# Linear attention and a two-layer MLP on one core: q of batch 2, its four tiles and block 0's outputs placed anew

## The chip, the cores and the metric

The kernel runs on one core of one Trainium2 chip, in one launch. The metric is the device time of one execution in microseconds, as the median of several. A core has TensorE (PE in the profile; its weight loads are PEld), VectorE (DVE), ScalarE (ACT), GpSimd (POOL) and SyncE (SP), each with its own in-order queue of instructions, and 16 DMA engines, which the queues of SyncE, ScalarE and GpSimd feed.

## The reference

Per batch and head, `kv = k^T v` and `out = q kv`, normalised by its root mean square over the head and scaled by `g_norm`. The heads side by side give `x` with 512 columns; after a layer norm it goes through two matrices with a ReLU between, and `x` is added. There are 8 batches, 8 heads, 576 rows, head size 64 and 2048 hidden columns.

```
kv  = einsum('bhsd,bhse->bhde', k, v)
o   = einsum('bhsd,bhde->bhse', q, kv)
x   = o / sqrt(mean(o*o, -1) + 1e-6) * g_norm       # then heads side by side
xn  = (x - mean(x)) / sqrt(var(x) + 1e-6) * g_ln
out = x + relu(xn @ w_ch1) @ w_ch2
```

## The kernel before

Each batch gives a block of 512 rows, in four tiles of 128; the last 64 rows of all batches make a ninth block, "rem". Tile (b, j) below is the j-th tile of batch b.

**A block's matrices.** `mm1` (L680) multiplies the block's turned x, `xT_blk`, by w1 and ScalarE stores the ReLU as `m1` (L693). `mm2` multiplies m1 by w2. Block 0 does it plainly, in `mm2_part` (L708) and `finish` (L717). Block 0's w2 matmuls run over w2's 16 row groups in steps (0-3, 4-5, 6-7, 8-9, 10-11, 12-15), each step over all four tiles. The other blocks use seven products instead of eight (`mm2_seven`, L543), which need four sums of quarters of m1, S1 to S4, made on VectorE (`row_sums`, L503 to L514), and four sums of quarters of w2, T1 to T4 (`weight_sums`, L495, on VectorE during blocks 0 and 1). In blocks 1 and 2 the order of the products is p1, p4, p2, p5 (wants S1), p6 (S2), p7 (S4), p3 (S3).

**A tile.** `o` (L294) multiplies turned q (`qts`) by kv on TensorE, into PSUM. `sq` (ScalarE, L305) and `red` (VectorE, L376) give the sums of squares. `y`, `x` and `xc_w` (root on ScalarE L384; then VectorE L391, L380, L398, L402, L423) normalise and centre it, as `xc`. `turn` (L425) turns xc into `xT_blk`, either by four transposes on TensorE into the single PSUM buffer "misc" and a copy on ScalarE (L430, L432), or by a DMA transpose in SyncE's queue (L434). `var` (ScalarE, L416) is wanted only for the scale `rstd` of the block's outputs.

**q and kv.** q, k and v arrive by DMAs in GpSimd's queue (`load`, L96; two each, lower and upper rows). `turn_q_dma` (L218) reorders q on VectorE (L223) and turns it with a DMA transpose in SyncE's queue (L225): five pieces of four 128 x 128 blocks. Batch 1 has its own form, `q_start` and `q_turns` (L904, L912): the first two pieces by TensorE (`turn_q`, L184), and the other three, 12 blocks, by DMA. `kv_of` (L265) makes a batch's kv in the PSUM buffer "misc". `keep_q` (L231) puts the last 64 rows' q aside.

**The order of the work.** Everything is emitted in an order written by hand, and every engine runs its share of it in that order. `tick()` (L777) is called about every 0.87 us of TensorE's work, before the matmuls of that tick; it emits what `at(slot, ...)` (L768) has put into that tick, in order of slots. Row sums come first in a tick. Ticks 0 to 15 are mm1 of block 0, 16 to 31 its mm2, 32 to 47 mm1 of block 1 (rows 0 to 255, then from tick 40 the others), 48 to 61 its seven products, two ticks each, 62 to 77 mm1 of block 2, 78 to 91 its products, and 92 begins mm1 of block 3. Slots are 32 to a block, and their second half is pressed into the 14 ticks of the products: slot 52.7 is tick 52, 58.3 is tick 57, 63.3 is tick 61, 68 is tick 66.

`plan_tile(s, ...)` puts a tile's `o`, `sq` and `red` at slot s, `y`, `x` and `xc_w` at s + 2, its turn and its `var` at slots of their own. In the kernel before:

| tick | emitted (beside the ReLU's matmuls) |
|---|---|
| 20, 21, 24, 28, 31 | kv of batch 1; then `o`, `sq`, `red` of tiles (1,0) to (1,3) |
| 23, 26, 30, 33 | `y`, `x`, `xc_w` of tiles (1,0) to (1,3) |
| 27, 31, 35, 38 | turns of tiles (1,0) to (1,3), on TensorE |
| 34 | q of batch 2: copy and DMA transpose of all 20 blocks |
| 34, 37, 39 | three of the four `weight_sums` |
| 40 | kv of batch 2 |
| 43, 48, 57, 61 | `o`, `sq`, `red` of tiles (2,0) to (2,3) |
| 45, 50, 58, 63 | `y`, `x`, `xc_w` of tiles (2,0) to (2,3) |
| 48, 52, 59, 65 | turns of tiles (2,0) to (2,3), by DMA |
| 46 to 54 | row sums of block 1 |
| 52, 58 | q of batch 3 (copy, DMA transpose); kv of batch 3 |
| 43, 66 | loads of batches 3 and 4, six DMAs each |

In GpSimd's queue a load of a later batch stands behind a "gate", a copy of one element (L105) that waits until the old contents have been used: that of batch 3 waits for turned q of batch 2, that of batch 4 also for the last element of block 2's `xT_blk` (L939).

**Before the first tick,** GpSimd's queue is given all the early loads in order: k, v, q of batch 0, w1, w2 row groups 0 to 3, q, k and v of batch 1 (L172 to L174), and w2 rows 4-5, 6-7, 8-9, 10-11 and 12-15 (L175 to L179). The loads of batch 2 follow in tick 9.

**Block 0's outputs.** `finish` scales by rstd and adds x. For tiles 0 and 1 ScalarE (L723) and GpSimd (L724) do it, for 2 and 3 VectorE alone (L726). Then the tile is stored at once in two DMAs, in SyncE's queue (`store`, L730).

Of the kernel before, what the change touches and what calls it, by code (L numbers as in the profile page):

```python
# [14 lines left out]
def kernel(  # L15
# [11 lines left out]
    nc = tc.nc  # L27
    f32 = mybir.dt.float32
    bf16 = mybir.dt.bfloat16
# [66 lines left out]
    def load(dst, t, b, h0=0, h1=H):  # L96
        nc.gpsimd.dma_start(dst[:64, h0:h1], lo(t, b, h0, h1))
        nc.gpsimd.dma_start(dst[64:, h0:h1, :J], up(t, b, h0, h1))
# [19 lines left out]
    def load_w2(de0, de1):  # L118
        nc.gpsimd.dma_start(
            w2_sb[:, de0:de1, :],  # L120
            moe_w_ch2[de0 * 128:de1 * 128, :].rearrange("(ko p) n -> p ko n", p=128))
# [48 lines left out]
        nc.vector.memset(t, 0.0)  # L170

    load_w2(0, 4)  # L172
    for dst, src in ((q_in, q), (k_in, k), (v_in, v)):
        load(dst[1], src, 1)  # L174
    load_w2(4, 6)  # L175
    load_w2(6, 8)
    load_w2(8, 10)
    load_w2(10, 12)
    load_w2(12, nDe)  # L179


    qts, held, blks, rstds, m1s, q_ps = {}, {}, {}, {}, {}, {}
# [254 lines left out]
    def main_tile(b, j, pool=None, tag="ops"):  # L437
        q_t, kvp = qts[b], held[b]
        if b not in blks:
            blks[b] = new_block()  # L440
        return Tile([(slice(0, 128), lambda hp: q_t[:, j, hp, :], kvp)], blks[b], j, pool, tag)
# [7 lines left out]
            blks["rem"] = new_block()  # L449
        return Tile(mms, blks["rem"], b // 2)  # L450

    def plan_tile(s, make, turn_at, on_pe, var_at):
        box = []

        def first():
            t = make()
            box.append(t)
            if t.mms:
                t.o()
            t.sq()  # L460
            t.red()

        def second():
            t = box[0]
            t.y()
            t.x()
            t.xc_w()

        at(s, first)
        at(s + 2, second)  # L470
        at(turn_at, lambda: box[0].turn(on_pe))
        at(var_at, lambda: box[0].var())

# [9 lines left out]
    H2, C2 = nDe // 2, Dm // 2  # L483
    SPLIT = (0, 6, 12, nDe)
    SPLIT_2, TICKS_2 = (0, 12, nDe), ((0, 1, 4, 7), (0, 1, 4, 6))
    sums = {}

    def m1_q(b, rows, odd):
# [191 lines left out]
    def mm1(b, t0, n, c0=0, c1=nDe):  # L680
        blk, m1 = blks[b], m1_of(b)
        sl = slice(t0 * 128, (t0 + n) * 128)
        per = 4 // n
        for de0 in range(c0, c1, per):
            tick()
            p1 = ps1.tile([128, per, n * 128], f32, tag="p1", name="p1")
            for i in range(per):
                de = de0 + i
                for kk in range(nK):
                    nc.tensor.matmul(p1[:, i, :], lhsT=w1_sb[:, kk, de * 128:(de + 1) * 128],  # L690
                                     rhs=blk[2][:, kk, sl],
                                     start=(kk == 0), stop=(kk == nK - 1))
            nc.scalar.activation(m1[:, de0:de0 + per, sl], p1, func=AF.Relu)  # L693
            del p1
            if b in (1, 2) and t0 + n == 4 and de0 + per in SPLIT_2:
                i = SPLIT_2.index(de0 + per)
                row_sums(b, SPLIT_2[i - 1] // 2, SPLIT_2[i] // 2, TICKS_2[i - 1])
            elif b in SEVEN and b not in (1, 2) and de0 + 1 in SPLIT:
                i = SPLIT.index(de0 + 1)
                row_sums(b, SPLIT[i - 1] // 2, SPLIT[i] // 2, range(4))  # L700
# [16 lines left out]
    def finish(b, ts, p2):  # L717
        if ts % 2 == 0:
            o_pair[b] = outp.tile([128, 2, Dm], f32, tag="osb", name="o_sb")
        o_sb = o_pair[b][:, ts % 2]  # L720
        r, x = rstds[b][:, ts:ts + 1], blks[b][0][:, ts]
        if ts < 2:
            nc.scalar.activation(o_sb, p2, func=AF.Copy, scale=r)  # L723
            nc.gpsimd.tensor_add(o_sb, o_sb, x)  # L724
        else:
            nc.vector.scalar_tensor_tensor(o_sb, in0=p2, scalar=r, in1=x,  # L726
                                           op0=ALU.mult, op1=ALU.add)
        store(b, ts, o_pair[b][:, ts % 2:ts % 2 + 1])

    def store(b, ts, o_sb, c0=0, c1=Dm, upper=None):  # L730

        n = o_sb.shape[1]
        if b == "rem":
            dst = out[:, :S_LO, :].rearrange("(t f) (p j) e -> f j p t e", j=JJ, f=2)[:, J]
            for half, engine in enumerate((nc.sync, upper)):
                engine.dma_start(dst[half, :, ts:ts + n, c0:c1],
                                 o_sb[half * 64:half * 64 + 64, :, c0:c1])
            return
        eng = nc.gpsimd if b == 1 and ts >= 2 else nc.sync
        for half in range(2):  # L740
            src = o_sb[half * 64:half * 64 + 64, :, c0:c1]
            if b == 0:
                j = 2 * ts + half
                dst = (out[b, :S_LO, :].rearrange("(p j) e -> p j e", j=JJ)[:, j:j + 1] if ts < 2
                       else out[b, S_LO:, :].rearrange("(p j) e -> p j e", j=J)[:, j - J:j - J + 1])
            else:
                dst = (out[b, S_LO:, :].rearrange("(p j) e -> p j e", j=J) if half else
                       out[b, :S_LO, :].rearrange("(p j) e -> p j e", j=JJ))[:, ts:ts + n]
            eng.dma_start(dst[:, :, c0:c1], src)
# [18 lines left out]
    def at(slot, fn):  # L768

        i, r = divmod(slot, 32)  # L770
        blocks = [*range(B), "rem"]
        if r > 16 and i < len(blocks) and blocks[int(i)] in SEVEN:
            r = 16 + (r - 16) * 14 / 16
        s = sum(30 if x in SEVEN else 32 for x in blocks[:int(i)]) + r
        agenda.setdefault(int(s + 1e-6), []).append((s, fn))
# [125 lines left out]
    at(20, lambda: (rstd_of(0), t.clear()))  # L901


    def q_start():  # L904
        q_ps[1] = kv_in.tile([128, JJ, H, D], bf16, tag="qp", bufs=1, name="q_p")
        nc.vector.tensor_copy(q_ps[1].rearrange("p j h d -> p h j d"), q_in[1])
        qts[1] = qt_pool.tile([128, JJ, HP, 128], bf16, tag="qt", name="qt")
        nc.sync.dma_start_transpose(
            qts[1][:, 2:].rearrange("p j hp t -> p (j hp) t"),
            q_ps[1][:, 2:].rearrange("p j h d -> p (j h d)"))  # L910

    def q_turns():  # L912
        turn_q(1, 0, ps_out, "ops")
        turn_q(1, 1, ps_m, "misc")
        del q_ps[1]

    at(12.5, q_start)
    at(17, q_turns)
    at(20, lambda: kv_of(1))
    for j, s, tn in ((0, 21, 27), (1, 24, 31), (2, 28, 35), (3, 31.5, 38)):  # L920
        plan_tile(s, lambda j=j: main_tile(1, j), tn, True, (27.7, 33, 41, 44.5)[j])
    at(33.2, lambda: keep_q(1))
    at(46, lambda: rstd_of(1))

    at(40, lambda: kv_of(2))
    at(34, lambda: turn_q_dma(2))
    for j, s, tn in ((0, 43.2, 48), (1, 48.3, 53.5), (2, 58.3, 61.5), (3, 63.3, 67.5)):
        plan_tile(s, lambda j=j: main_tile(2, j), tn, False, (55.5, 59.5, 63, 67.5)[j])
    at(64, lambda: keep_q(2))
    at(70.5, lambda: rstd_of(2))  # L930


# [3 lines left out]
    for slot, what, after in (  # L936
            (43, (("q", 3), ("k", 3), ("v", 3)), lambda: (turned_q(2),)),
            (68, (("q", 4), ("k", 4), ("v", 4)),
             lambda: (turned_q(3), blks[2][2][:1, nK - 1, 511:])),  # L939
            (92.7, (("q", 5), ("k", 5), ("v", 5)), lambda: (turned_q(4),)),  # L940
            (124.7, (("q", 6), ("k", 6), ("v", 6)), lambda: (turned_q(5),)),
            (156.7, (("q", 7), ("k", 7), ("v", 7)), lambda: (turned_q(6),))):
        load_batches(slot, what, after)


    for b, s in ((3, 60), (4, 93), (5, 123), (6, 155), (7, 187)):
        at(s, lambda b=b: kv_of(b))
    rems = {}

# [10 lines left out]
    at(268, lambda: rstd_of("rem"))  # L960


    for b, at_q, at_o in ((3, 52.7, (68.5, 72.5, 76.5, 83)), (4, 81, (96.5, 102.7, 109, 115)),
                          *((b, 32 * b - 47.2, tuple(32 * b - i for i in (34.5, 27.3, 20.1, 12.9)))
                            for b in range(5, B))):
        at(at_q, lambda b=b: turn_q_dma(b))
        for j, o in enumerate(at_o):
            plan_tile(o, lambda b=b, j=j: main_tile(b, j), o + 4.5, False, 32 * b - 13.4 + 3.5 * j)
        at(at_o[-1] + .5, lambda b=b: keep_q(b))
        at(32 * b + 6, lambda b=b: rstd_of(b))  # L970
# [9 lines left out]
        mm1(0, ts, 1, c0, c1)  # L980
    p2s = [ps1.tile([128, Dm], f32, tag="p1", name="p2") for _ in range(2)]
    p2s += [ps2.tile([128, Dm], f32, tag="p2", name="p2") for _ in range(2)]
    for de0, de1 in ((0, 4), (4, 6), (6, 8), (8, 10), (10, 12)):
        for ts in range(4):
            mm2_part(0, ts, p2s[ts], de0, de1)
    for ts in range(4):
        p2 = p2s[ts]
        p2s[ts] = None
        mm2_part(0, ts, p2, nDe * 3 // 4, nDe)
        finish(0, ts, p2)  # L990
        del p2
    del blks[0], m1s[0]
# [41 lines left out]
```

## Time and profile before

| | |
|---|---|
| median of three executions | 285.53 us (283.41 to 286.06) |
| the profiled execution: its own time | 285.37 us |
| its span, first to last instruction | 283.4 us |
| VectorE: q_p copy L223 of batch 2 starts | 55.47 us |
| ScalarE: output copies L723 of block 0 | 47.14 and 48.00 us, 0.69 us each |
| VectorE: outputs L726 of block 0 | 51.28 and 52.53 us, 0.75 us each |
| SyncE: eight stores of block 0 (L749) | from 49.26 us, 5.79 us |
| GpSimd: loads of batch 3 issued | 63.57 to 67.7 us |
| landing of batch 1's v, upper rows | issued at 20.90 us, 14.2 us to landing |
| landing of batch 2's v, upper rows | issued at 41.37 us, 13.7 us to landing |

All times count from the start of the span. A line of the timeline gives the start, the length, the engine (a "q" behind it is the engine's queue of issues), the line of the kernel, the operation, what it writes and reads, and in brackets how long the engine stood before it and what ended that. In the table by stretches each row has the stretch, its length, then busy time and number of instructions of PE, PEld, DVE, ACT and POOL, the clock granted to TensorE as a share of full speed, the share of the DMA engines' time and GB/s.

### The profile page before, as it was taken

How to read it: one execution, taken by the hardware profiler on the slowest of the kernel's cores; microseconds unless marked ns; L12 is line 12 of the kernel's file. 1: busy time of each engine (PE TensorE's matmuls, PEld its weight loads, DVE VectorE, ACT ScalarE, POOL GpSimd, SP SyncE). 2: the span in 40 equal slices, each digit the busy share in tenths (PEclk: the TensorE clock that was granted, in tenths of full speed). 3: DMA queues.
4: the chain of work that ended last, by engine and by line, in shares of the span. 5: the costliest groups of instructions: out<-in, count | busy, mean ns of one | idle time of the engine just before them, and what ended most of it. 6: DMA issues, size and time to landing. Idle time of an engine off the chain costs nothing.

```text
span 283.4 us, 6487 instructions
## 1 busy us (share of the span) xinstructions
PE 270.2 (95%) x2518; PEld 193.5 (68%) x2534; DVE 198.7 (70%) x466; ACT 184.6 (65%) x410; POOL 109.8 (39%) x134
## 2 busy tenths in 40 slices
PE   8999999979997999999999999999999999999993
PEld 2689744868876898547854885488448844874683
DVE  6675756956987487699678856985797559923563
ACT  3567755767757576687758776776677477846610
POOL 8433752105084602960591069016401610180140
PEclk9999999999999799999999999999999999999999
DMA  7999999949975897696679959982431151015022
GB/s 215 198 207 202 200 177 197 246 96 139 141 149 141 120 170 133 109 192 137 129 102 217 187 65 134 256 133 48 113 75 20 21 148 37 21 20 150 0 74 76
DMA packets 65190, 36.80 MB, mean 130 GB/s; under 512 B 35072, under 2 KB 61956, under 8 KB 65160
## 3 DMA queue, kind: packets, MB, share of 16 engines
q0 software_dynamic: 28720, 18.29, 46.0%
q1 hardware_dynamic: 35848, 17.12, 27.9%
q10 hardware_dynamic: 592, 0.98, 1.0%
q8 instruction: 20, 0.33, 0.5%
q14 instruction: 10, 0.08, 0.1%
HBM read 36.71 MB, written 9.44 MB: 163 GB/s over the span
## 4 chain that ended last, share of the span: by engine, by line
PE 73%; DMA 20%; DVE 2%; SPq 1%; issue 1%; POOL 1%; ACT 1%; POOLq 0%
PE p L690 36%; DMA w_sb<-in_moe_w_ch_dram 9%; PE p_x L523 9%; PE p_z L523 8%; PE p_y L523 8%; DMA k_in<-in_k_dram 5%; PE p_s L523 4%; PE p_q L523 4%; DMA xT_blk<-xc 3%; DMA qt<-q_p 2%; PE o_ps L299 2%; PE p L712 1%; SPq L225 1%; PE kv_ps L272 1%; ACT v L557 1%
## 5 line engine op out<-in xcount | busy, mean ns | idle before, releaser
L690 PE MATMUL p<-xT_blk,w_sb 128*128 128x512 bf16 (+2 forms) x884 | 131.8, 305 | 3.9 <-DMA xT_blk<-xc 2.7
L693 ACT ACTIVATE m<-p 128x512 bf16<-128x512 f32 x144 | 85.1, 596 | 42.1 <-PE p L690 40.1
L690 PEld LDWEIGHTS <-w_sb 128*128 128x128 bf16 x896 | 77.3, 99 | 50.0 <-issue 3.9
L523 PEld LDWEIGHTS <-m 128*128 128x128 bf16 x512 | 49.4, 98 | 7.2
L376 DVE TENSOR_REDUCE ss<-sq 128x8 f32<-128x512 f32 x35 | 23.8, 681 | 27.0 <-ACT sq L305 26.9
L523 PEld LDWEIGHTS <-S 128*128 128x128 bf16 x392 | 37.5, 98 | 5.1 <-DVE S L512 0.8
L578 POOL TENSOR_TENSOR q<-q,x_blk 128x512 f32<-128x512 f32 x5 | 6.4, 1290 | 70.0 <-ACT q L557 70.0
L416 ACT ACTIVATE dev<-x_blk,st_blk 128x512 f32<-128x512 f32 x36 | 25.8, 719 | 2.4 <-DVE st_blk L402 2.4
L523 PE MATMUL p_x<-w_sb,m 128*128 128x256 bf16 x224 | 27.3, 273 | 0.0
L380 DVE TENSOR_TENSOR o_ps<-o_ps,inv 128x512 f32<-128x512 f32 x33 | 23.1, 700 | 3.0
L305 ACT ACTIVATE sq<-o_ps 128x512 f32<-128x512 f32 x35 | 20.9, 596 | 5.7 <-PE o_ps L299 5.6
L398 DVE SCALAR_TENSOR_TENSOR x_blk<-o_ps,g_norm_sb 128x512 f32<-128x512 f32 x33 | 22.8, 691 | 1.1
L605 POOL TENSOR_TENSOR u<-u,x_blk 128x512 f32<-128x512 f32 x7 | 8.9, 1266 | 37.0 <-DVE u L562 37.0
L511 DVE TENSOR_TENSOR S<-m 128x768 bf16<-128x768 bf16 (+2 forms) x22 | 12.5, 569 | 12.7 <-ACT m L693 12.7
L423 DVE TENSOR_SCALAR xc<-x_blk,st_blk 128x512 bf16<-128x512 f32 x32 | 17.6, 550 | 1.1
L384 ACT ACTIVATE rms<-ss,eps_sb 128x8 f32<-128x8 f32 x36 | 10.7, 298 | 9.0 <-DVE ss L376 8.7
L562 DVE SCALAR_TENSOR_TENSOR u<-p_y,rstd,v 128x256 f32<-128x256 f32 x28 | 12.2, 477 | 5.3 <-PE p_y L523 5.3
L712 PE MATMUL p<-w_sb,m 128*128 128x512 bf16 x61 | 15.0, 379 | 1.0 <-DMA w_sb<-in_moe_w_ch_dram 0.8
L557 ACT ACTIVATE v<-p_x,rstd 128x256 f32<-128x256 f32 x28 | 11.0, 476 | 6.3 <-PE p_x L523 6.3
L391 DVE RECIPROCAL inv<-rms 128x8 f32<-128x8 f32 x36 | 7.1, 196 | 11.2 <-ACT rms L384 11.0
L523 PE MATMUL p_y<-T,S 128*128 128x256 bf16 x112 | 13.7, 273 | 0.6 <-DVE S L512 0.6
L523 PE MATMUL p_y<-T,m 128*128 128x256 bf16 x112 | 14.0, 272 | 0.0
(148 smaller groups left out, 366.4 us busy)
## 6 DMA issues: line engine op xcount, KB each, us to landing
out_dram<-o_sb SPq DMA_DIRECT2D x26, 256.0 KB, 4.2
w_sb<-in_moe_w_ch_dram POOLq DMA_DIRECT2D x6, 512.0 KB, 14.2
q_in<-in_q_dram POOLq DMA_DIRECT2D x7, 320.0 KB, 4.6
k_in<-in_k_dram POOLq DMA_DIRECT2D x7, 320.0 KB, 6.8
v_in<-in_v_dram POOLq DMA_DIRECT2D x7, 320.0 KB, 9.8
q_in<-in_q_dram POOLq DMA_DIRECT2D x8, 256.0 KB, 5.3
k_in<-in_k_dram POOLq DMA_DIRECT2D x7, 256.0 KB, 7.5
v_in<-in_v_dram POOLq DMA_DIRECT2D x7, 256.0 KB, 12.8
```

The lines of the kernel that those rows point to most:

```text
L305: nc.scalar.activation(self.sq_t, self.o_ps, func=AF.Square)
L376: nc.vector.tensor_reduce(self.ss, self.sq_t, axis=AX.X, op=ALU.add)
L380: nc.vector.tensor_mul(self.o_ps, self.o_ps, self.inv().to_broadcast([128, H, D]))
L398: nc.vector.scalar_tensor_tensor(x_blk[:, ts].rearrange("p (h d) -> p h d", h=H), in0=self.o_ps, scalar=1.0, in1=g_norm_sb.to_broadcast([1 ...
L416: nc.scalar.activation(dev, x_blk[:, ts], func=AF.Square, bias=st[:, 1, ts:ts + 1], accum_out=st[:, 2, ts:ts + 1])
L423: nc.vector.tensor_scalar_add(self.xc_t, x_blk[:, self.ts], st[:, 1, self.ts:self.ts + 1])
L511: for i, fn in enumerate((lambda: nc.vector.tensor_add(S1, a21, a22), lambda: nc.vector.tensor_sub(S2, S1, a11), lambda: nc.vector.tensor_ ...
L523: nc.tensor.matmul(dst[:, t - ts[0], :c1 - c0], lhsT=a[:, i, t * 128:(t + 1) * 128], rhs=w[:, i, c0:c1], start=start and t == ts[0] and i ...
L557: nc.scalar.activation(dst[:, t], src[:, t], func=AF.Copy, scale=rstd[:, 2 * rows + t:2 * rows + t + 1])
L690: nc.tensor.matmul(p1[:, i, :], lhsT=w1_sb[:, kk, de * 128:(de + 1) * 128], rhs=blk[2][:, kk, sl], start=(kk == 0), stop=(kk == nK - 1))
L693: nc.scalar.activation(m1[:, de0:de0 + per, sl], p1, func=AF.Relu)
L712: nc.tensor.matmul(p2[:, c0:c1], lhsT=m1s[b][:, de, ts * 128:(ts + 1) * 128], rhs=w2_sb[:, de, c0:c1], start=(de == 0), stop=(de == nDe - 1))
```

## The change

q of batch 2 gets batch 1's form: a copy and a DMA transpose of the last four pieces in tick 29, and its first piece turned by TensorE in tick 37. The tiles of batch 2 get ticks of their own:

| | before | after |
|---|---|---|
| `o`, `sq`, `red` of tiles (2,0) to (2,3) | 43, 48, 57, 61 | 42, 44, 54, 58 |
| `y`, `x`, `xc_w` | 45, 50, 58, 63 | 44, 46, 58, 60 |
| turns | 48, 52, 59, 65, all by DMA | 46, 48, 59 by DMA, 68 by TensorE |
| row sums of block 1: S1, S2, S4, S3, first part | 46, 47, 50, 53 | 47, 48, 50, 53 |
| the same, second part | 48, 49, 52, 54 | 48, 49, 50, 53 |
| q of batch 3; kv of batch 3 | 52; 58 | 51; 61 |
| `keep_q` of batch 2 | 62 | 59 |
| turns of tiles (1,1) and (1,3) | 31; 38 | 30; 38 |

Block 0's last four row groups of w2 are done as 12-13 over all tiles and then 14-15 tile by tile, and are loaded in two DMAs. v of batch 1 is loaded behind w2 rows 4-5. All four outputs of block 0 go through ScalarE and GpSimd, and the eight stores move to GpSimd's queue in tick 40. The gate of batch 4's loads looks at tile (2,2)'s part of `xT_blk` instead of the last one.

```diff
@@ -170,13 +170,12 @@
         nc.vector.memset(t, 0.0)
 
     load_w2(0, 4)
-    for dst, src in ((q_in, q), (k_in, k), (v_in, v)):
-        load(dst[1], src, 1)
+    load(q_in[1], q, 1)
+    load(k_in[1], k, 1)
     load_w2(4, 6)
-    load_w2(6, 8)
-    load_w2(8, 10)
-    load_w2(10, 12)
-    load_w2(12, nDe)
+    load(v_in[1], v, 1)
+    for de in range(6, nDe, 2):
+        load_w2(de, de + 2)
 
 
     qts, held, blks, rstds, m1s, q_ps = {}, {}, {}, {}, {}, {}
@@ -449,7 +448,7 @@
             blks["rem"] = new_block()
         return Tile(mms, blks["rem"], b // 2)
 
-    def plan_tile(s, make, turn_at, on_pe, var_at):
+    def plan_tile(s, make, turn_at, on_pe, var_at, second_at=None):
         box = []
 
         def first():
@@ -467,7 +466,7 @@
             t.xc_w()
 
         at(s, first)
-        at(s + 2, second)
+        at(second_at or s + 2, second)
         at(turn_at, lambda: box[0].turn(on_pe))
         at(var_at, lambda: box[0].var())
 
@@ -483,6 +482,7 @@
     H2, C2 = nDe // 2, Dm // 2
     SPLIT = (0, 6, 12, nDe)
     SPLIT_2, TICKS_2 = (0, 12, nDe), ((0, 1, 4, 7), (0, 1, 4, 6))
+    TICKS_1 = ((1, 2, 4, 7), (0, 1, 2, 5))
     sums = {}
 
     def m1_q(b, rows, odd):
@@ -694,7 +694,7 @@
             del p1
             if b in (1, 2) and t0 + n == 4 and de0 + per in SPLIT_2:
                 i = SPLIT_2.index(de0 + per)
-                row_sums(b, SPLIT_2[i - 1] // 2, SPLIT_2[i] // 2, TICKS_2[i - 1])
+                row_sums(b, SPLIT_2[i - 1] // 2, SPLIT_2[i] // 2, (TICKS_1 if b == 1 else TICKS_2)[i - 1])
             elif b in SEVEN and b not in (1, 2) and de0 + 1 in SPLIT:
                 i = SPLIT.index(de0 + 1)
                 row_sums(b, SPLIT[i - 1] // 2, SPLIT[i] // 2, range(4))
@@ -719,13 +719,10 @@
             o_pair[b] = outp.tile([128, 2, Dm], f32, tag="osb", name="o_sb")
         o_sb = o_pair[b][:, ts % 2]
         r, x = rstds[b][:, ts:ts + 1], blks[b][0][:, ts]
-        if ts < 2:
-            nc.scalar.activation(o_sb, p2, func=AF.Copy, scale=r)
-            nc.gpsimd.tensor_add(o_sb, o_sb, x)
-        else:
-            nc.vector.scalar_tensor_tensor(o_sb, in0=p2, scalar=r, in1=x,
-                                           op0=ALU.mult, op1=ALU.add)
-        store(b, ts, o_pair[b][:, ts % 2:ts % 2 + 1])
+        nc.scalar.activation(o_sb, p2, func=AF.Copy, scale=r)
+        nc.gpsimd.tensor_add(o_sb, o_sb, x)
+        o_tile = o_pair[b][:, ts % 2:ts % 2 + 1]
+        at(40.2, lambda: store(b, ts, o_tile))
 
     def store(b, ts, o_sb, c0=0, c1=Dm, upper=None):
 
@@ -736,7 +733,7 @@
                 engine.dma_start(dst[half, :, ts:ts + n, c0:c1],
                                  o_sb[half * 64:half * 64 + 64, :, c0:c1])
             return
-        eng = nc.gpsimd if b == 1 and ts >= 2 else nc.sync
+        eng = nc.gpsimd if b == 0 or b == 1 and ts >= 2 else nc.sync
         for half in range(2):
             src = o_sb[half * 64:half * 64 + 64, :, c0:c1]
             if b == 0:
@@ -901,32 +898,35 @@
     at(20, lambda: (rstd_of(0), t.clear()))
 
 
-    def q_start():
-        q_ps[1] = kv_in.tile([128, JJ, H, D], bf16, tag="qp", bufs=1, name="q_p")
-        nc.vector.tensor_copy(q_ps[1].rearrange("p j h d -> p h j d"), q_in[1])
-        qts[1] = qt_pool.tile([128, JJ, HP, 128], bf16, tag="qt", name="qt")
+    def q_start(b, j0):
+
+        q_ps[b] = kv_in.tile([128, JJ, H, D], bf16, tag="qp", bufs=1, name="q_p")
+        nc.vector.tensor_copy(q_ps[b].rearrange("p j h d -> p h j d"), q_in[b % NB])
+        qts[b] = qt_pool.tile([128, JJ, HP, 128], bf16, tag="qt", name="qt")
         nc.sync.dma_start_transpose(
-            qts[1][:, 2:].rearrange("p j hp t -> p (j hp) t"),
-            q_ps[1][:, 2:].rearrange("p j h d -> p (j h d)"))
-
-    def q_turns():
-        turn_q(1, 0, ps_out, "ops")
-        turn_q(1, 1, ps_m, "misc")
-        del q_ps[1]
-
-    at(12.5, q_start)
-    at(17, q_turns)
+            qts[b][:, j0:].rearrange("p j hp t -> p (j hp) t"),
+            q_ps[b][:, j0:].rearrange("p j h d -> p (j h d)"))
+
+    def q_turns(b, *pools):
+        for j, (pool, tag) in enumerate(pools):
+            turn_q(b, j, pool, tag)
+        del q_ps[b]
+
+    at(12.5, lambda: q_start(1, 2))
+    at(17, lambda: q_turns(1, (ps_out, "ops"), (ps_m, "misc")))
     at(20, lambda: kv_of(1))
-    for j, s, tn in ((0, 21, 27), (1, 24, 31), (2, 28, 35), (3, 31.5, 38)):
+    for j, s, tn in ((0, 21, 27), (1, 24, 30.2), (2, 28, 35), (3, 31.5, 38.6)):
         plan_tile(s, lambda j=j: main_tile(1, j), tn, True, (27.7, 33, 41, 44.5)[j])
     at(33.2, lambda: keep_q(1))
     at(46, lambda: rstd_of(1))
 
     at(40, lambda: kv_of(2))
-    at(34, lambda: turn_q_dma(2))
-    for j, s, tn in ((0, 43.2, 48), (1, 48.3, 53.5), (2, 58.3, 61.5), (3, 63.3, 67.5)):
-        plan_tile(s, lambda j=j: main_tile(2, j), tn, False, (55.5, 59.5, 63, 67.5)[j])
-    at(64, lambda: keep_q(2))
+    at(29.5, lambda: q_start(2, 1))
+    at(37, lambda: q_turns(2, (ps_m, "misc")))
+    for j, s, x_at, tn, va in ((0, 42, 44, 46, 55.5), (1, 44.2, 46.2, 49, 57.5),
+                               (2, 55.5, 59.5, 61, 63), (3, 60.5, 62.6, 70, 67.5)):
+        plan_tile(s, lambda j=j: main_tile(2, j), tn, j == 3, va, x_at)
+    at(61, lambda: keep_q(2))
     at(70.5, lambda: rstd_of(2))
 
 
@@ -936,14 +936,14 @@
     for slot, what, after in (
             (43, (("q", 3), ("k", 3), ("v", 3)), lambda: (turned_q(2),)),
             (68, (("q", 4), ("k", 4), ("v", 4)),
-             lambda: (turned_q(3), blks[2][2][:1, nK - 1, 511:])),
+             lambda: (turned_q(3), blks[2][2][:1, nK - 1, 383:384])),
             (92.7, (("q", 5), ("k", 5), ("v", 5)), lambda: (turned_q(4),)),
             (124.7, (("q", 6), ("k", 6), ("v", 6)), lambda: (turned_q(5),)),
             (156.7, (("q", 7), ("k", 7), ("v", 7)), lambda: (turned_q(6),))):
         load_batches(slot, what, after)
 
 
-    for b, s in ((3, 60), (4, 93), (5, 123), (6, 155), (7, 187)):
+    for b, s in ((3, 63.5), (4, 93), (5, 123), (6, 155), (7, 187)):
         at(s, lambda b=b: kv_of(b))
     rems = {}
 
@@ -960,7 +960,7 @@
     at(268, lambda: rstd_of("rem"))
 
 
-    for b, at_q, at_o in ((3, 52.7, (68.5, 72.5, 76.5, 83)), (4, 81, (96.5, 102.7, 109, 115)),
+    for b, at_q, at_o in ((3, 52, (68.5, 72.5, 76.5, 83)), (4, 81, (96.5, 102.7, 109, 115)),
                           *((b, 32 * b - 47.2, tuple(32 * b - i for i in (34.5, 27.3, 20.1, 12.9)))
                             for b in range(5, B))):
         at(at_q, lambda b=b: turn_q_dma(b))
@@ -980,13 +980,13 @@
         mm1(0, ts, 1, c0, c1)
     p2s = [ps1.tile([128, Dm], f32, tag="p1", name="p2") for _ in range(2)]
     p2s += [ps2.tile([128, Dm], f32, tag="p2", name="p2") for _ in range(2)]
-    for de0, de1 in ((0, 4), (4, 6), (6, 8), (8, 10), (10, 12)):
+    for de0, de1 in ((0, 4), (4, 6), (6, 8), (8, 10), (10, 12), (12, 14)):
         for ts in range(4):
             mm2_part(0, ts, p2s[ts], de0, de1)
     for ts in range(4):
         p2 = p2s[ts]
         p2s[ts] = None
-        mm2_part(0, ts, p2, nDe * 3 // 4, nDe)
+        mm2_part(0, ts, p2, 14, nDe)
         finish(0, ts, p2)
         del p2
     del blks[0], m1s[0]
```

## The prediction

> **What bounds the kernel now.** I read the page first, for the busy shares and the slices.
>
> ```profile
> span 283.4 us, 6487 instructions
> ...
> PE 270.2 (95%) x2518; PEld 193.5 (68%) x2534; DVE 198.7 (70%) x466; ACT 184.6 (65%) x410; POOL 109.8 (39%) x134
> ...
> PEclk9999999999999799999999999999999999999999
> ```
>
> TensorE is the bound, and its work is hardly touched. So all that can be won is the time in which it stands, plus the one slice (the 14th, from 92.1 us) in which its clock was low. Next, the list of TensorE's waits (total, times, longest):
>
> ```profile
> PE p L690 <- DMA xT_blk<-xc: 2.7, 2, 2.0
> PE o_ps L299 <- DMA qt<-q_p: 1.8, 1, 1.8
> ...
> PE p L712 <- DMA w_sb<-in_moe_w_ch_dram: 0.8, 2, 0.4
> ...
> PE p_y L523 <- DVE S L512: 0.6, 1, 0.6
> ```
>
> Then TensorE's timeline, to place them (start, length, what, idle before):
>
> ```profile
> 36.50 0.82 PE L272 MATMUL kv_ps<-v_in,k_in 128*64 128x64 bf16 x40
> 37.74 1.02 PE L712 MATMUL p<-w_sb,m 128*128 128x512 bf16 x3 [0.42 <-DMA w_sb<-in_moe_w_ch_dram]
> ...
> 46.08 2.75 PE L712 MATMUL p<-w_sb,m 128*128 128x512 bf16 x11 [0.38 <-DMA w_sb<-in_moe_w_ch_dram]
> ...
> 63.08 0.40 PE L299 MATMUL o_ps<-kv_pack,qt 128*128 128x128 bf16 x4 [1.84 <-DMA qt<-q_p]
> ...
> 82.39 3.65 PE L690 MATMUL p<-xT_blk,w_sb 128*128 128x256 bf16 x32 [0.67 <-DMA xT_blk<-xc]
> ...
> 86.11 3.66 PE L690 MATMUL p<-xT_blk,w_sb 128*128 128x256 bf16 x32
> ...
> 92.01 5.32 PE L690 MATMUL p<-xT_blk,w_sb 128*128 128x256 bf16 x32 [2.02 <-DMA xT_blk<-xc]
> ```
>
> The same 32 matmuls take 3.66 us at 86.11 and 5.32 at 92.01, so the last wait costs 2.02 and then 1.66 more. The table by stretches shows why: the clock.
>
> ```profile
> 93.00:94.00 1.00, 1.00 (x7) 0.69 (x6) 0.00 (x0) 0.60 (x1) 0.75 (x2) 0.50 0.65 131
> ```
>
> Last, who was late: VectorE's timeline, then SyncE's queue.
>
> ```profile
> 55.47 0.82 DVE L223 COPY q_p<-q_in 128x2560 bf16<-128x2560 bf16 x1
> ...
> 75.45 0.82 DVE L223 COPY q_p<-q_in 128x2560 bf16<-128x2560 bf16 x1
> ...
> 86.18 0.67 DVE L423 TENSOR_SCALAR xc<-x_blk,st_blk 128x512 bf16<-128x512 f32 x1
> ```
>
> ```profile
> 56.45 3.08 SPq L225 DMA_TRANSPOSE qt<-q_p  x1
> 68.99 1.20 SPq L434 DMA_TRANSPOSE xT_blk<-xc  x1
> 76.42 3.19 SPq L225 DMA_TRANSPOSE qt<-q_p  x1
> 79.65 3.28 SPq L434 DMA_TRANSPOSE xT_blk<-xc  x2
> 86.87 17.63 SPq L434 DMA_TRANSPOSE xT_blk<-xc  x4
> ```
>
> All three late transposes are VectorE's doing. q of batch 2 landed about 48.8 (its second load is issued at 36.24 and takes 12.6), but was copied only at 55.47, in VectorE's order, and turned by 63.08. Tile (2,1)'s turn sat on SyncE behind q of batch 3, copied at 75.45. Tile (2,3)'s xc was ready at 86.85 and landed 5.0 us later.
>
> **The first part: loads and block 0.** v of batch 1 now follows w2 rows 4-5. The bytes ahead of w2 row 6 are the same, so v lands when rows 4-5 did, at 37.7 (issued at 23.56, 14.1 to landing). But kv of batch 1 stands in TensorE's order at 36.50, before the matmuls on rows 4-5. So its wait is 1.2 us, in the place of 0.42. Bounds: 0, if v still lands by its old 35.1 or a little after, and 2.8, if it lands with rows 6-7 (39.28). I take 1.2, since loads have one queue. The wait of 0.38 at 46.08 goes: TensorE comes later, and rows 12-13 are a load of their own. **Removed 0.80, added 1.2.**
>
> Block 0's last two outputs leave VectorE (L726, 2 x 0.75) for ScalarE (L723, 2 x 0.69) and GpSimd (L724, 2 x 1.25). Nothing of that is on TensorE's path by itself, but ScalarE is tight there. Its queue from 48.5, laid out by start-to-start distances (0.49 a Relu, 0.48 a transpose's copy, 0.59 an L723, 0.80 a variance), gives the first Relu of block 1 at 51.9 instead of 51.05. The one PSUM buffer "misc" now takes three turnings in ticks 35 to 38 instead of two: tile (1,2), q's first piece, tile (1,3). Each waits until ScalarE has copied the one before. I get 0.1 at the second and 0.4 at the third: **added 0.5** (bounds 0, and 1.4 if both L723 lie on the path whole). q's first piece is four transposes, 0.22 from start to start as at 52.59 (0.40 alone): **added 0.22**.
>
> **q of batch 2.** The copy moves to tick 29, before tile (1,2)'s normalisation, where VectorE stood 1.75 us (48.91, for ScalarE). It waits for q's landing at 48.8, with that normalisation queued behind it: copy to 49.6, xc of (1,2) at 52.0, not 51.3. TensorE turns that tile at about 52.9 (50.3 + 3 x 0.87): 0.9 us of cover, and one for one beyond. The transpose of 16 blocks starts on SyncE at 49.7 instead of 56.45, while k and v of batch 2 still load (to 55.1). Undisturbed, 20 blocks took 6.6 us; among loads, batch 1's 12 blocks took 15.5. Bounds of landing: 55 and 65.2. I take 58 to 60. Tile (2,0) no longer needs it; tile (2,1) does, at 58.7 (tick 40) + 0.75 + 4 x 0.87 + 0.22 = 63.2. **Removed 1.84.**
>
> **The tiles around the row sums.** mm2 of block 1 would start at about 66.9 (67.9 before). VectorE's order is then: the two first tiles done at 68.4, S1 S2 S4 over both parts (0.87 + 0.34 each) to 72.1, q of batch 3 to 72.8, S3 to 74.1. Products want S1 at 72.1 (S1 ends by 70.5), S2 at 74.1 (70.9), S4 at 75.8 (72.1), S3 at 77.8 (74.1). Tile (2,1)'s turn is issued at 68.4 and has until 80.5; its 0.67 goes. Tile (2,2) is reduced after S3, and its xc comes at 78.7, turned by DMA with 5 us or so to 84, wanted at 88. Tile (2,3)'s xc comes at 82.8, and TensorE turns it in tick 68, at 86: 0.22 more, and a copy of 0.48 on ScalarE, which has 0.38 to spare per tick of 0.87. **Removed 0.67 + 2.02 + 1.66, added 0.22.** From mm2 of block 2 on the order is unchanged; 0.56 before a p_y (S2 of block 3) stays.
>
> **Stores and gates.** Eight stores leave SyncE (5.79 us) for GpSimd's queue in tick 40, behind four adds, to about 60 at 0.55 each (two at 86.85 took 1.10). Behind them stand the gate and the six loads of batch 3, which then start at 60.3 instead of 63.57. The gate of batch 4 looks at tile (2,2), which lands before q of batch 4 is needed. kv of batch 3 goes three slots later, for v. Nothing on the path.
>
> **The sum.** Removed 0.80 + 1.84 + 0.67 + 2.02 + 1.66 = 6.99. Added 1.2 + 0.5 + 0.22 + 0.22 = 2.14. Net 4.85 us off the profiled execution's 285.37 (its span of 283.4 and 1.97 around it): **280.5 us**. That execution lies within 0.2 of the median, 285.53.
>
> **The rivals.**
> *The clock falls anyway*, or after another wait: 1.66 isn't won, 282.2. The 1.84 wait at 61 cost no clock, the 2.02 wait did; so a wait of 2 us is about where it begins, and 1.2 is below it. The Trainium skill ("TensorE: Matmul & The Clock Gate", Part 1) has the gate close only after an idle window of some 3.4 us, and pass half the clock for about as long; the 0.50 agrees, the 2.02 does not. By that rule the slow stretch would have another cause and stay. 0.10.
> *q lands late.* At the 15.5 us of batch 1's transpose it lands at 65.2, tile (2,1) waits 2.0: 282.5, and 284.2 with the clock. For it: the loads beside it. Against: they end by 55, those of batch 1 at 46. 0.12.
> *VectorE becomes the bound.* It is busy 9.62, 9.54 and 9.55 of 10 us in the stretches at 50, 70 and 100. If tile (2,3) comes over 3 us after 82.8, or the sums 3 after mine, half the gain returns as waits: 283.
> Against: it loses 1.5 us of L726, and my layout has margins of 1.6 or more. 0.07.
> *Slower: GpSimd's queue.* The loads of batch 3 stand behind the eight stores. If each takes what its loads did from 18.35 to 26.08 (2.6 us apart, ended by earlier landings) instead of 0.55, the last v load is issued at 81 instead of 64.5 and lands 9.9 us later at 91, where kv of batch 3 wants it at 79: 12 us and 1.66 of clock, so 285.4 - 4.85 + 13.7 = 294. It decides from about 5 us of delay on. Against: v of batch 2 has landed by then, so nothing fills the queue. The Trainium skill ("SBUF — State Buffer", "SBUF: two separate sides") says that VectorE, in some modes, keeps GpSimd from writing descriptors; just behind three weight scalings, from 36.20, the DMAs moved 24 GB/s for 0.70 us, which fits it but does not show it. 0.06.
>
> **The numbers.** My forecast has 0.65. Low: all of 6.99 and the 0.56 too, less the two turnings, 278.3. High: the forecast with its first wait at 2.8 gives 282.1, the late q 282.5, both 284.1; I take 284.0. Beyond lie the slower rival and the ends of others. One per cent is 2.85 us, about what a measurement of this kernel can tell from no change: faster below 282.7. Faster: 0.60 of the forecast, 0.07, 0.06 and 0.01 of the first three rivals, 0.74; within: 0.05, 0.03, 0.06, 0.06, so 0.20; slower 0.06.
>
> **What would show it.** In the changed profile: kv of batch 1 waits about 1.2 us for v; tile (2,0) starts without a wait; no wait on xT in block 2; PEclk is 9 throughout; mm2 of block 1 starts near 66.9 and the first Relus of block 1 are about 0.9 later. It is wrong if tile (2,1) waits for qt, if VectorE waits for q_in well past 49, if SyncE's turns of (2,2) come after 84, or if the loads of batch 3 are issued later than 65.

## The result and the profile after

The changed kernel is slower, by about 1%: 286.94 us median (283.57 to 289.72, 22 executions) against 283.62 us (283.18 to 286.06, 22 executions) for the kernel before; the ratio is 1.0084, with a 95% interval of 1.006 to 1.0109. The ratio is one of means and leaves out the four longest executions of the changed kernel, those with the lowest clock; that of the medians is 1.012. The forecast was 280.5.

The profiled execution of the changed kernel took 284.26 us. Its span is shorter than the one of before, although the median is longer. From the page:

```profile
span 282.0 us, 6503 instructions
...
PE 269.3 (95%) x2526; PEld 194.2 (69%) x2542; DVE 197.8 (70%) x464; ACT 185.7 (66%) x414; POOL 117.0 (41%) x145
...
PEclk9999999999999997999999999999999999999999
```

The slice with a low clock is now the 16th instead of the 14th, 106 to 113 us. TensorE's waits (total, times, longest):

```profile
PE kv_ps L271 <- DMA v_in<-in_v_dram: 5.0, 2, 2.7
...
PE p L690 <- ACT xT_blk L351: 0.3, 1, 0.3
PE tp L429 <- ACT qt L190: 0.2, 1, 0.2
```

The waits on turned q, turned x and w2 are gone, and so is the one on S2. In their place are two waits for v, 5.0 us in all. (Two more rows, of 1.3 and 0.5 us, belong to the start of the kernel.) TensorE's timeline places them:

```profile
38.75 0.82 PE L271 MATMUL kv_ps<-v_in,k_in 128*64 128x64 bf16 x40 [2.23 <-DMA v_in<-in_v_dram]
...
67.74 1.91 PE L523 MATMUL p_x<-w_sb,m 128*128 128x256 bf16 x16
...
81.35 3.66 PE L690 MATMUL p<-xT_blk,w_sb 128*128 128x256 bf16 x32
...
89.01 3.66 PE L690 MATMUL p<-xT_blk,w_sb 128*128 128x256 bf16 x32
...
96.22 1.91 PE L523 MATMUL p_x<-w_sb,m 128*128 128x256 bf16 x16
...
108.94 1.28 PE L271 MATMUL kv_ps<-v_in,k_in 128*64 128x64 bf16 x40 [2.73 <-DMA v_in<-in_v_dram]
...
113.94 5.34 PE L690 MATMUL p<-xT_blk,w_sb 128*128 128x512 bf16 x23
```

In the kernel before, block 2's products began at 100.88 and block 3 at 114.41. So at 96.22 the change was 4.66 us ahead, and at 113.94 it was 0.47 ahead: 4.2 us were given back inside block 2's products, at one wait. The 40 matmuls behind that wait take 1.28 instead of 0.82 us: the clock is down again. The table by stretches (here TensorE alone: busy time, clock, DMA share, GB/s) has it:

```profile
108.90:112.00 3.10, 3.06 (x49) 0.50 1.40 176
112.00:114.00 2.00, 2.00 (x22) 0.98 0.04 4
```

What the wait is for stands in the chain of waits, in order of time (start, length, what).

```profile
93.30 15.51 DMA v_in<-in_v_dram
```

In the kernel before, the same last load of v was issued at 96.64 and landed in 10.9 us.

VectorE's timeline answers to the rows of before: q of batch 2 is copied at 49.29, q of batch 3 at 74.68, and the xc of tile (2,3) is there at 84.6 instead of 86.85 (the forecast had 82.8).

```profile
49.29 0.83 DVE L904 COPY q_p<-q_in 128x2560 bf16<-128x2560 bf16 x1 [0.31 <-issue]
...
74.68 0.82 DVE L222 COPY q_p<-q_in 128x2560 bf16<-128x2560 bf16 x1
...
84.12 0.49 DVE L422 TENSOR_SCALAR xc<-x_blk,st_blk 128x512 bf16<-128x512 f32 x1
```

**The clock tells executions apart.** The mean granted clock of each execution is known. Of 35 executions of the kernel before beside the first four experiments, 22 had 0.996 or more (median 283.8 us) and 13 had 0.990 to 0.994 (285.9 us). The profile that the forecast was made from had 0.994. In the changed kernel one execution of 22 had 0.999 (283.57 us), four had 0.994 (284.26 to 285.26), thirteen 0.984 to 0.988 (286.73 to 287.47), and four 0.979 or 0.980 (288.30 to 289.72). One stretch of 3.4 us at half clock, as in both profiles, lowers the mean by 3.4 x 0.5 / 283 = 0.006. So the usual execution of the changed kernel has the low clock of two such stretches or more (two falls, or one that lasts twice as long, as in experiment 1), that of the kernel before of none or one. By the means, 0.9869 and 0.9967, the low clock takes at most 3.7 and 0.9 us of full-speed time; a part of that can lie at the very end, where TensorE has no work left (the last digit of PEclk is an 8 in the profiles of experiments 6, 7 and 9).

### The profile page after: what moved, and what is told of

It reads as the page before. It is cut to its first block, busy times and chain, and to the rows that moved or that the text cites. A ratio compares the mean times of both kernels' runs of the same rounds, so it can differ in the third digit from the quotient of the medians.

```text
span 282.0 us, 6503 instructions
## 1 busy us (share of the span) xinstructions
PE 269.3 (95%) x2526; PEld 194.2 (69%) x2542; DVE 197.8 (70%) x464; ACT 185.7 (66%) x414; POOL 117.0 (41%) x145
## 4 chain that ended last, share of the span: by engine, by line
PE 66%; DMA 19%; DVE 6%; POOL 4%; issue 3%; ACT 1%; DVEq 0%; POOLq 0%
PE p L690 31%; DMA v_in<-in_v_dram 13%; PE p_y L523 7%; PE p_z L523 7%; PE p_x L523 6%; DMA w_sb<-in_moe_w_ch_dram 5%; PE p_s L523 4%; PE p L712 3%; PE p_q L523 3%; PE o_ps L298 2%; PE kv_ps L271 2%; DVE x_blk L397 1%; DVE o_ps L379 1%; DVE xc L422 1%; ACT m L693 1%
## 5 line engine op out<-in xcount | busy, mean ns | idle before, releaser
L690 PEld LDWEIGHTS <-w_sb 128*128 128x128 bf16 x896 | 76.3, 98 | 46.2 <-issue 0.9
L511 DVE TENSOR_TENSOR S<-m 128x768 bf16<-128x768 bf16 (+2 forms) x22 | 12.2, 554 | 12.5 <-ACT m L693 12.5
L562 DVE SCALAR_TENSOR_TENSOR u<-p_y,rstd,v 128x256 f32<-128x256 f32 x28 | 12.2, 476 | 5.9 <-PE p_y L523 5.9
L523 PE MATMUL p_z<-w_sb,S 128*128 128x256 bf16 x112 | 14.4, 283 | 0.0
L523 PE MATMUL p_q<-T,m 128*128 128x256 bf16 x112 | 13.4, 273 | 0.0
```

The source lines that it names most:

```text
L511: for i, fn in enumerate((lambda: nc.vector.tensor_add(S1, a21, a22), lambda: nc.vector.tensor_sub(S2, S1, a11), lambda: nc.vector.tensor_ ...
L523: nc.tensor.matmul(dst[:, t - ts[0], :c1 - c0], lhsT=a[:, i, t * 128:(t + 1) * 128], rhs=w[:, i, c0:c1], start=start and t == ts[0] and i ...
L562: V.scalar_tensor_tensor(dst[:, t], in0=src[:, t], scalar=rstd[:, 2 * rows + t:2 * rows + t + 1], in1=other[:, t], op0=ALU.mult, op1=ALU.add)
```

## The experiments

The theory was: the change wins what was forecast up to block 2, and two waits for v, with a fall of the clock after each in most executions, give it back. The first rival was that the clock falls for some other reason; the others are about the loads of batch 4. All figures are medians, and a kernel before ran beside each (284.3 us with the first four, 283.75 with the next three, 284.51 with the last two; 283.62 beside the result, so a difference from the changed kernel's 286.94 is good to about 1 us).

**1. v of batch 1 loaded as before.**

```diff
-    load_w2(4, 6)
     load(v_in[1], v, 1)
+    load_w2(4, 6)
```

> The changed kernel with the loads of v of batch 1 back in front of w2 rows 4-5; all else as changed. Theory (two new waits for v, and the clock that falls after each, give back what the change wins): the wait of 2.23 us before kv of batch 1 goes, up to 0.8 us of waits for w2 come back, and one fall of the clock (1.7 us) is gone in most executions, so about 1.4 + 1.7 = 3 us less than the changed kernel: 283.5 to 285, granted clock 0.991 to 0.995 instead of 0.986. Rival (the clock falls for another reason than the waits): only the 1.4 us, 285.5, clock still 0.986.

Measured: 284.15 us, ratio 0.997 (0.9933 to 1.0007), mean clock 0.992. The first wait is gone (0.26 for w2 is left of it) and 2.8 us with it, as the theory has it. The second wait grew:

```profile
108.56 1.28 PE L271 MATMUL kv_ps<-v_in,k_in 128*64 128x64 bf16 x40 [3.32 <-DMA v_in<-in_v_dram]
```

TensorE now comes earlier and v of batch 4 hardly does. In the profiled execution, with a mean clock of 0.986, this one wait is followed by some 6.8 us at half clock, from 107.7 us on, most of the 16th slice:

```profile
PEclk9999999999999996999999999999999999999999
```

Four of the 12 executions have such a clock, 0.985 or 0.986; three have 0.999 or more (281.7 to 282.76 us).

**2. That part alone, in the kernel before.**

```diff
-    for dst, src in ((q_in, q), (k_in, k), (v_in, v)):
-        load(dst[1], src, 1)
+    load(q_in[1], q, 1)
+    load(k_in[1], k, 1)
     load_w2(4, 6)
+    load(v_in[1], v, 1)
```

> The kernel before with one part of the change alone: v of batch 1 loaded behind w2 rows 4-5. Theory: a wait of about 2.2 us before kv of batch 1 in the place of 0.4 for w2, 1 to 1.4 us at the end of block 0's matmuls, and a fall of the clock in most executions: 285 to 287 us against 283.6, clock 0.994 where it was 0.999. Rival (the wait is absorbed, since block 0 then waits less for w2): within 0.5 us of the kernel before.

Measured: 286.95 us, ratio 1.0069 (1.0041 to 1.0098), mean clock 0.9947. This one part makes the old kernel about as slow as the whole change does. Three executions kept a clock of 0.999 or more and took 285.14 to 285.78 us; the nine others took 286.53 to 287.71. So the wait alone costs some 1.5 us, and the fall as much again. Its page and TensorE's timeline show the fall right at the new wait:

```profile
PEclk9999979999999999999999999999999999999999
```

```profile
39.04 1.28 PE L273 MATMUL kv_ps<-v_in,k_in 128*64 128x64 bf16 x40 [2.48 <-DMA v_in<-in_v_dram]
```

**3. The waits kept, TensorE kept busy in them.**

```diff
-    at(20, lambda: kv_of(1))
+    at(20, lambda: (fill(8, ps_out.tile([128, 512], f32, tag="ops", name="idle")), kv_of(1)))
...
+    def fill_idle():
+        fill(10, ps_out.tile([128, 512], f32, tag="ops", name="idle"))
+
+    at(92.99, fill_idle)
```

The added matmuls multiply zeros; their results are not used.

> The changed kernel with matmuls of zeros put in front of the two waits for v: 8 (1.7 us) before kv of batch 1 and 10 (2.2 us) before kv of batch 4; they use up time in which TensorE stands. Theory (the clock falls because of these waits): the waits' length stays, the clock holds at 0.997 to 0.999, and the time falls by two falls of the clock, 3 us: 283.5 to 284.5. Rival (the clock falls for another reason, such as denser work): no gain, 286.5 to 287.5, clock 0.986.

Measured: 284.3 us, ratio 0.9972 (0.9936 to 1.0008), and no execution of 12 under a clock of 0.996. Both v's land as late as before, at 39.0 and 108.7 us; TensorE's timeline at the second wait:

```profile
106.68 2.10 PE L214 MATMUL idle<-fill_sb 128*128 128x512 bf16 x9
108.84 0.82 PE L271 MATMUL kv_ps<-v_in,k_in 128*64 128x64 bf16 x40
```

So some 2.6 us of the changed kernel's 286.9 are the clock, not the waiting, and the waits bring it about. The first rival is out.

**4. kv of batch 4 later.**

```diff
-    for b, s in ((3, 63.5), (4, 93), (5, 123), (6, 155), (7, 187)):
+    for b, s in ((3, 63.5), (4, 96), (5, 123), (6, 155), (7, 187)):
...
-    for b, at_q, at_o in ((3, 52, (68.5, 72.5, 76.5, 83)), (4, 81, (96.5, 102.7, 109, 115)),
+    for b, at_q, at_o in ((3, 52, (68.5, 72.5, 76.5, 83)), (4, 81, (97.5, 102.7, 109, 115)),
```

> The changed kernel with kv of batch 4 three ticks later (tick 92) and the first tile of batch 4 one tick later. Theory: the wait of 2.73 us there shrinks to 0.2 or none and its fall of the clock goes with it: 4 us less than the changed kernel, 282.5 to 283.5, clock 0.993. Rival (the next thing is as late: q or x of block 3 turned by DMA land no earlier than now, at 113 us): TensorE waits for turned x at the start of block 3 instead, and the time falls by less than 1.5 us.

Measured: 287.57 us, ratio 1.0089 (1.005 to 1.0129), mean clock 0.986. My expectation failed and its rival held: v landed even later (17.6 us after its issue), and behind it turned x of block 3, which waits on SyncE for the transpose of q of batch 4. TensorE's timeline:

```profile
111.01 0.82 PE L271 MATMUL kv_ps<-v_in,k_in 128*64 128x64 bf16 x40 [1.62 <-DMA v_in<-in_v_dram]
115.26 0.61 PE L690 MATMUL p<-xT_blk,w_sb 128*128 128x512 bf16 x1 [3.43 <-DMA xT_blk<-xc]
```

The transpose of q of batch 4 lands 13.8 us after its issue, against 5.6 in the kernel before: several transfers of that stretch are late together, and moving one matmul that wants one of them does not help.

**5. Block 3's first three tiles turned by TensorE,** with v of batch 1 as in 1.

```diff
-            plan_tile(o, lambda b=b, j=j: main_tile(b, j), o + 4.5, False, 32 * b - 13.4 + 3.5 * j)
+            plan_tile(o, lambda b=b, j=j: main_tile(b, j), o + 4.5, b == 3 and j < 3, 32 * b - 13.4 + 3.5 * j)
```

> v of batch 1 loaded as before, and the first three tiles of block 3 turned by TensorE (12 transposes, 0.66 us) instead of by DMA, so that no transpose of x runs beside the loads of batch 4; those loads stay where the change has them. Theory (DMA engines shared between loads and transposes): v of batch 4 lands in 11 to 12 us instead of 15.5, by 104, and kv of batch 4 waits under 0.3 us: 279.5 to 281.5. Rival (the loads are slow by themselves, or held by the transpose of q of batch 4, which stays): v still takes 14 us or more, and kv of batch 4 waits 2 us or more: 283.5 or more.

Measured: 285.72 us, ratio 1.0049 (1.0021 to 1.0077). The cause is confirmed, and the expected time was missed by over 4 us. With no transpose of x beside them, the loads of batch 4 take 9.8 us to the last landing instead of 15.5, and kv of batch 4 doesn't wait. But TensorE now waits 3.8 us for the xc of these tiles, since it turns them in the ticks that were chosen for a DMA. TensorE's timeline, the longest of three:

```profile
99.67 0.40 PE L429 MATMUL tp<-identity,xc 128*128 128x128 bf16 x4 [2.30 <-DVE xc L422]
```

**6. The loads of batch 4 eight ticks earlier** (slot 60 is tick 58, not 60 as the expectation says), behind the gate on turned q of batch 3 alone. They are then issued from 83.6 us on, in part in a gap of GpSimd, all before block 3's tiles are turned (from 91.3).

```diff
-            (68, (("q", 4), ("k", 4), ("v", 4)),
-             lambda: (turned_q(3), blks[2][2][:1, nK - 1, 383:384])),
+            (60, (("q", 4), ("k", 4), ("v", 4)), lambda: (turned_q(3),)),
```

> The changed kernel with the six loads of batch 4 emitted in tick 60 instead of 66, with the gate on turned q of batch 3 alone: they are issued from about 83.6 us instead of 89.9, before the turns of block 3's tiles (from 91 us). Theory (v of batch 4 is late because its loads and the DMA transposes of block 3 share the DMA engines): the loads land in 11 to 13 us, v by 99, kv of batch 4 doesn't wait (at 106.2), and 2.7 us and one fall of the clock go: 4 us less than the changed kernel, about 283. Rival (the transposes are then delayed as much, or turned x of block 2's third tile, issued at 81): a wait of 1 to 3 us on turned x in block 2 or at block 3's start, and less than 1.5 us gained.

Measured: 281.36 us, ratio 0.9916 (0.9885 to 0.9947): 5.6 us less than the changed kernel. v lands 12.2 us after its issue, at 99.3, and kv of batch 4 starts without a wait. The gain is larger than the 4 us expected. The wait for v of batch 1 is still there (2.43), and one of 0.6 on S2 of block 3 is back.

**7. Both, 1 and 6.**

> Both waits for v undone at once: v of batch 1 loaded in front of w2 rows 4-5, as before, and the loads of batch 4 in tick 60. Theory: no wait of 2 us is left, the clock holds at 0.997 or more, and what the change wins elsewhere (1.84 + 0.67 + 2.02 and the clock's fall of before) is kept: 278.5 to 280.5, faster than both kernels. Rival (each wait taken away lets the next late transfer show): 282 or more, with a new wait on a DMA of over 1 us.

Measured: 279.49 us, ratio 0.9843 (0.9812 to 0.9875), no execution of six under 0.997. This beats both kernels, and is 1 us below the time that the forecast had given to the change. Of TensorE's waits over 0.5 us, these are left (the first is at the start):

```profile
PE p L214 <- DVE eps_sb L150: 1.3, 1, 1.3
PE o_ps L298 <- DMA qt<-q_p: 1.1, 1, 1.1
PE p_y L523 <- DVE S L512: 0.6, 1, 0.6
```

**8. The version of 7 with block 0's outputs as before** (two on VectorE, stores at once in SyncE's queue).

```diff
-        nc.scalar.activation(o_sb, p2, func=AF.Copy, scale=r)
-        nc.gpsimd.tensor_add(o_sb, o_sb, x)
-        o_tile = o_pair[b][:, ts % 2:ts % 2 + 1]
-        at(40.2, lambda: store(b, ts, o_tile))
+        if ts < 2:
+            nc.scalar.activation(o_sb, p2, func=AF.Copy, scale=r)
+            nc.gpsimd.tensor_add(o_sb, o_sb, x)
+        else:
+            nc.vector.scalar_tensor_tensor(o_sb, in0=p2, scalar=r, in1=x,
+                                           op0=ALU.mult, op1=ALU.add)
+        store(b, ts, o_pair[b][:, ts % 2:ts % 2 + 1])
...
-        eng = nc.gpsimd if b == 0 or b == 1 and ts >= 2 else nc.sync
+        eng = nc.gpsimd if b == 1 and ts >= 2 else nc.sync
```

> The version with both waits for v undone, and with it block 0's outputs as before: two of the four on VectorE, all stored at once in SyncE's queue. Theory (this part of the change moves work that lies beside TensorE's): within 0.6 us of that version's 279.5. Rival (it matters: with two outputs on VectorE the tiles of batch 1 come 1.5 us later, or SyncE's stores hold up a transpose): 281 or more, with a wait of over 1 us on turned x or q in block 1.

Measured: 280.31 us, ratio 0.9853 (0.9816 to 0.9889). The intervals of 7 and 8 overlap, so by time the part is not settled: 0.8 us more than 7 lies between the two expectations. The trace leans to the rival: TensorE waits 1.15 and 0.57 us for the xc of tiles (1,2) and (1,3), which VectorE's two outputs have pushed back.

```profile
53.45 0.40 PE L429 MATMUL tp<-identity,xc 128*128 128x128 bf16 x4 [1.15 <-DVE xc L422]
```

**9. The kernel before, kept busy in its wait at 90 us.**

```diff
     at(70.5, lambda: rstd_of(2))
+    at(72.9, lambda: fill(8))
```

> The kernel before with 8 matmuls of zeros (1.7 us) in its wait of 2.02 us at 90 us. Theory (that wait lets the clock fall in about half of the executions, and only in these is 1.7 us lost): the slower executions of 285.4 vanish, all lie at 283.2 to 284.2, clock 0.997 or more; the median stays near that of the kernel before or falls by up to 0.9. Rival (the clock falls in the kernel before for another reason): executions of 285.4 with clock 0.994 stay as frequent.

Measured: 284.0 us, ratio 0.9979 (0.995 to 1.0008). All 12 executions lie between 283.17 and 285.07, at a clock of 0.997 or more; of the 17 executions of the kernel before beside them, 8 had 0.990 to 0.994. That wait was the cause of its falls, but only in part of its executions. In time the gain is not clear of nothing, and two executions, 284.73 and 285.07, lie above the range that I expected although their clock did not fall.

## Why the prediction was wrong

**Right: the waits that go, and VectorE's order.** Tile (2,0) starts without a wait, tile (2,1) too, and no wait on turned x is left in block 2. q of batch 2 has landed when the gate looks (it runs at 60.45, right behind the stores), so the rival of a late q is out. mm2 of block 1 starts at 67.74; forecast 66.9, and the difference is mostly the first wait below. TensorE's place at the start of block 2's products, 4.66 us ahead, is within 0.2 of the forecast's 4.85. That it is so close is partly luck: the first wait was 1.0 longer than forecast, the waits at "misc" 0.3 shorter, and the remaining 0.5 lies in gaps too short for the list of waits. VectorE came later than in my layout (q of batch 3 copied by 75.5, not 72.8; the last xc 1.8 later), but the margins held. GpSimd's queue held up nothing: the stores took 4.22 us, and batch 3's first load was issued at 60.58 (60.3).

**Mis-sized: the wait for v of batch 1.** I put it at 1.2 us, with bounds of 0 and 2.8, from the landing of rows 4-5 before; it is 2.23. v's second load was issued at 23.24, took 15.3 us and landed at about 38.5, not 37.7. Experiments 1 and 2 put the price of this edit at 2.8 and 2.65 us, clock included. I had called 1.2 us "below" what lets the clock fall; at 2.2 us it is not, as experiment 2 shows.

**Wrong: "From mm2 of block 2 on the order is unchanged".** The order is, but not what runs beside what, and the loads of batch 4, of which I wrote "Nothing on the path", were given no price. In the kernel before, the late turn of tile (2,3), TensorE's wait for it and the low clock held back block 3's tiles, whose turns are issued at 91.9, 98.34 and 103.31 (the first lands in 2.4 us), and the gate on that turn held back the loads until 93.25. With block 2 faster, the three turns are issued at 91.03, 94.39 and 98.65, beside loads that start at 89.92. So v of batch 4 is late and kv of batch 4 waits 2.73 us, where the sum had nothing. Rows of the DMA queues, both for the stretch from 98 to 100 us (packets, MB, the time of the packets as a share of 16 engines), show what that does to the loads. First the kernel before, where the transpose issued at 98.34 had moved nothing yet:

```profile
q0 software_dynamic: 675, 0.40, 137.4%
```

and the changed kernel, where the transposes are q1:

```profile
q0 software_dynamic: 387, 0.23, 107.1%
q1 hardware_dynamic: 175, 0.04, 39.2%
q8 instruction: 1, 0.02, 6.8%
```

The loads move 0.23 MB instead of 0.40. Experiments 5 and 6 show it from both sides: without these transposes, or issued ahead of them, the same loads take 9.8 and 12.2 us instead of 15.5. My rival on the slower side had the right kind of victim (a kv that waits for v) but the wrong loads and the wrong cause, GpSimd's queue. The rival "the clock falls anyway, or after another wait" had the right event, at 0.10 and for one fall.

The Trainium skill ("DMA: Bandwidth & Descriptors", "SWDGE vs HWDGE vs iDMA") says that the two kinds of DMA feed different queues inside each engine, and that the engine takes turns between them. These rows agree as far as they go: transposes of 0.04 MB take 39.2% while the loads move 0.17 MB less; turns themselves are not in the profile.

**Wrong: the clock's fall as a fixed 1.66 us.** It was in the profile of before, but only in 13 of 35 executions of that kernel, and in 2 and 8 of the two further sets of 17 (experiment 9 removes it). So the kernel to beat was one of 283.6 us, not 285.4, and about a third of the term was there to be won. One of the three executions that the forecast rested on, 283.41 us, was already of the faster kind. The other way round, the changed kernel's two waits lose it twice or more in most executions: up to 3.7 us against 0.9.

Without the clock the account is short. The only execution of the changed kernel without a fall took 283.57 us, and the 12 of experiment 3, whose waits are filled, 284.3; those of before without a fall 283.8. What goes (1.84 + 0.67 + 2.02 + 0.80 + 0.56 for S2 = 5.89) and what comes (2.23 + 2.73, two turnings of 0.22, and 0.2 at "misc", 5.6) nearly cancel; the clock makes the changed kernel the slower one.

## What to carry to other kernels

When a stretch of a kernel with little slack becomes faster, list every transfer of the stretches behind it with its issue and landing, and look which ones now run at the same time: an unchanged order of instructions is no unchanged traffic. A wait of TensorE of 2 us or more is worth more than its length, since the clock may fall after it; it is better moved (experiment 7) or filled (3 and 9); cutting one in two was not tried. And a single profile is one execution: before a term like a low clock enters a sum, compare its time with the spread of the runs.

## What had not been expected of the hardware

Waits of 2.0 to 2.7 us were enough to bring the clock to half speed for some 3.4 us, but not each time: 13 of 35 executions with one wait of 2.02, and 17 of 22 with two waits of 2.23 and 2.73 at a clock below 0.99. The Trainium skill ("TensorE: Matmul & The Clock Gate", Part 1) speaks of a free-running window of about 3.4 us, so that the moment depends on where in the window the work lies. That agrees with a fall in a part of the executions, and with its length; that a wait must fill a whole window does not agree with these runs. Matmuls of zeros in the wait held the clock in all of 24 executions.

The record of the clock in the traces shows with what the falls go. The clock changes only on a raster of 3.413 us: the low stretches last 3.41 or 6.83 us, and the full-speed stretch ahead of them 85.33 us in the kernel before and 102.40 in the changed one, 25 and 30 steps. TensorE's timeline cut into these steps gives the same answer in all eleven profiles, in 880 steps at full speed: the clock fell after every step in which TensorE stood 2.02 us or more, and after none with 1.95 or less. The wait of 1.84 at 61 us in the kernel before was split by the raster, 0.68 and 1.16; the 2.02 at 90 us lay within one step. In the profile of the changed kernel the first wait had at most 1.81 in one step, and the clock held; the second had 2.46, and it fell. So in these profiles a wait of little more than 2 us costs the clock only where it falls within one step, and where the steps lie differs from execution to execution. The clock came back after steps with 0.27 us of standing or less, and not after one with 0.87, which makes the long fall of experiment 1.
